# Rounding float64 weights to float32 without the second VectorE operation: bias taken off by ScalarE's scale, sign multiplied by GpSimd, no clamp

## The chip, the cores and the metric

The kernel runs on one core of a Trainium2 chip. A core has TensorE (PE in the profile: matmuls and transposes; PEld is its loading of weights), VectorE (DVE), ScalarE (ACT), GpSimd (POOL) and the DMA queues, here issued by SyncE (SP). Each engine works through its own instructions in program order and waits by semaphores for what other engines have to deliver first. The metric is the device time of one execution in microseconds (us), the median of several runs.

## The reference, cut to what matters

Attention in which each query keeps only its 32 largest scores, and behind it a feed-forward block with a gate:

```python
q, k, v: (8, 8, 576, 64) float32                    # batch, heads, sequence, head size
scores = (q @ k^T) / sqrt(64)
kth    = 32nd largest score of each row
attn   = softmax(where(scores >= kth, scores, -1e9))
x      = (attn @ v) laid out as (4608, 512)
g      = x @ w_gate                                 # w_gate, w_val: (512, 1536)
out    = (g * sigmoid(g) * (x @ w_val)) @ w_out     # w_out: (1536, 512)
```

`q`, `k` and `v` are float32. The three weights come out of NumPy as **float64**, because they are made by a product with a float64 number. The kernel computes in float32, so it has to round 2.36 million weights from 64 to 32 bits on the chip. That rounding is what the change is about.

## The kernel before

Work goes through the kernel in *units*: one unit is 128 queries of a pair of heads (both heads of 64 queries for the last rows). A unit's steps are spread over the engines and over later units, so that several units are in flight:

```python
def scores(n):      # TensorE: q k^T into PSUM; ScalarE: copies it to sc        (L304/L318, L309/L323)
def select(n):      # VectorE: top 32 by four rounds of max8 + match_replace    (L339, L343)
        nc.vector.tensor_scalar(                    # FAR for what lies below the 32nd        (L349)
            e[:, hs], sc[:, hs], m[:, t, TOP_K - 1 : TOP_K], FAR, ALU.is_lt, ALU.mult)
def penalize(n):    # GpSimd: e = e + sc                                        (L361)
def weigh(n):       # ScalarE: exp with row sums                                (L370)
def normalize(n):   # VectorE: reciprocal (L382); ScalarE: e * 1/sum            (L385)
def turn(n):        # TensorE: transposes of e (L397); ScalarE: copies (L398)
def values(n):      # TensorE: e v (L417, L426); ScalarE: copies to xT          (L441)
def feed(kb):       # feed-forward for 256 rows: L480 gate and value, L505-L513 on ScalarE and GpSimd,
                    # L526 or L566 with w_out; fed into the units' TensorE stream piece by piece
```

The rounding of the weights goes beside the first units. A piece is 128 x 512 weights; there are 24 pieces of `w_gate` and `w_val` and 12 of `w_out`. A float64 is two 32-bit words. The high word holds the sign, the 11 bits of the exponent and the upper 20 bits of the mantissa; the float32 needs those 20 bits and 3 more from the low word, rounded:

```python
def rounded(src, dst):
    w = ffn.tile([P, 2, WP, 2], I32, tag="w", name="w", bufs=3)
    nc.sync.dma_start(w[:].rearrange("p c f t -> p c (f t)"), src.bitcast(I32))           # L108
    yield
    low, high = w[:, :, :, 0], w[:, :, :, 1]
    size = conv.tile([P, 2, WP], FP32, tag="size", name="size", bufs=3)
    nc.scalar.activation(size[:], high.bitcast(FP32), AF.Abs)                              # L115
    nc.scalar.mul(low, low.bitcast(U32), 2.0**-29)         # top 3 bits, rounded            L117
    yield
    nc.gpsimd.tensor_scalar(size[:], size[:], HUGE, LEAST, ALU.min, ALU.max)               # L120
    yield
    bits = size[:].bitcast(I32)
    nc.vector.tensor_scalar(
        bits, bits, 3, 0x3FFFFFFF, ALU.logical_shift_left, ALU.bitwise_and)                # L124
    nc.gpsimd.tensor_tensor(bits, bits, low, ALU.add)                                      # L127
    yield
    nc.vector.scalar_tensor_tensor(                        # sign and top exponent bit
        out=dst.bitcast(I32), in0=high, scalar=-0x40000000, in1=bits,
        op0=ALU.bitwise_and, op1=ALU.bitwise_or)                                           # L130
```

`yield` parts a piece into stages. The stages of successive pieces are interleaved, a step of this loop after about every 2.2 of VectorE's selection instructions:

```python
    lags = (5, 3, 2, 2, 0)
    for n in range(2 * len(pieces) - 1 + lags[0]):
        for k, lag in enumerate(lags):
            if (n - lag) % 2 == 0:
                upto((n - lag) // 2, len(lags) - k)        # piece, stage
        ready[0] = max((n - lags[0]) // 2 + 1, 0)
        early[0] = lambda: upto(n // 2, 2)
        yield
```

`early[0]()` is called in each unit ahead of its exponentials, so that ScalarE's part of a piece need not wait behind them. The order of the rest of a unit:

```python
for n in range(NU + VALUES):
    ...
    penalize(n - 1); run(turn(n - 3)); finish_unit(n - 4)     # finish_unit calls values
    next(nxt, None)                  # scores(n + 1): TensorE
    early[0]()
    weigh(n - 1)
    run(nxt)                         # scores(n + 1): ScalarE's copies to sc
    dve(2, ...); pieces(2); dve(1); dve(1); run(norm); ...    # select(n), rounding, feed-forward pieces
```

Of the kernel before, what the change touches and what calls it, by code (L numbers as in the profile page):

```python
# [8 lines left out]
AF = mybir.ActivationFunctionType  # L9
ALU = mybir.AluOpType  # L10
FP32 = mybir.dt.float32
I32 = mybir.dt.int32
# [7 lines left out]
EPS = 1.0e-9  # L20
BLK = 256
WP = 256
HUGE = 122880.0
LEAST = 3.0517578125e-05


@with_exitstack
def kernel(
# [37 lines left out]
    nc = tc.nc  # L66
# [11 lines left out]
    scale = 1.0 / float(D) ** 0.5  # L78
# [26 lines left out]
    def rounded(src, dst):  # L105

        w = ffn.tile([P, 2, WP, 2], I32, tag="w", name="w", bufs=3)
        nc.sync.dma_start(  # L108
            w[:].rearrange("p c f t -> p c (f t)"), src.bitcast(I32)
        )  # L110
        yield
        low, high = w[:, :, :, 0], w[:, :, :, 1]

        size = conv.tile([P, 2, WP], FP32, tag="size", name="size", bufs=3)
        nc.scalar.activation(size[:], high.bitcast(FP32), AF.Abs)  # L115

        nc.scalar.mul(low, low.bitcast(U32), 2.0**-29)  # L117
        yield

        nc.gpsimd.tensor_scalar(size[:], size[:], HUGE, LEAST, ALU.min, ALU.max)  # L120
        yield

        bits = size[:].bitcast(I32)
        nc.vector.tensor_scalar(  # L124
            bits, bits, 3, 0x3FFFFFFF, ALU.logical_shift_left, ALU.bitwise_and
        )
        nc.gpsimd.tensor_tensor(bits, bits, low, ALU.add)  # L127
        yield

        nc.vector.scalar_tensor_tensor(  # L130
            out=dst.bitcast(I32), in0=high, scalar=-0x40000000, in1=bits,
            op0=ALU.bitwise_and, op1=ALU.bitwise_or,
        )

    def weights():


        pieces = []
        for f in range(0, DFF, WP):
            for src, dst in ((w_gate, wg), (w_val, wv)):  # L140
                for c in range(0, KC, 2):
                    rows = src[c * P : (c + 2) * P, f : f + WP]
                    pieces.append((
                        rows.rearrange("(c p) f -> p c f", p=P), dst[:, c : c + 2, f : f + WP]
                    ))
        for c in range(MC):
            pieces.append((
                w_out[c * P : (c + 1) * P].rearrange("p (c f) -> p c f", c=2),
                wo[:, c].rearrange("p (c f) -> p c f", c=2),
            ))  # L150
        pieces = [rounded(*p) for p in pieces]
        step = [0] * len(pieces)

        def upto(i, k):

            while 0 <= i < len(pieces) and step[i] < k:
                next(pieces[i], None)
                step[i] += 1


        lags = (5, 3, 2, 2, 0)
        for n in range(2 * len(pieces) - 1 + lags[0]):
            for k, lag in enumerate(lags):
                if (n - lag) % 2 == 0:
                    upto((n - lag) // 2, len(lags) - k)
            ready[0] = max((n - lags[0]) // 2 + 1, 0)
            early[0] = lambda: upto(n // 2, 2)
            yield
        early[0] = lambda: None


        add, sub = ALU.add, ALU.subtract
        lo, hi = slice(0, DM // 2), slice(DM // 2, DM)
        room = []
        for _ in range(3):
            t = ffn.tile([P, 4, DM // 2], FP32, tag="w", name="t", bufs=3)
            room += [t[:, 0:2], t[:, 2:4]]
        for m in range(0, MQ, 2):
            mm, nn = slice(m, m + 2), slice(MQ + m, MQ + m + 2)
            t3 = room.pop()  # L180
            nc.gpsimd.tensor_tensor(t3, wo[:, nn, hi], wo[:, mm, hi], sub)
            T[7] += [t3[:, i, :] for i in range(2)]
            yield
        while not plain_done:
            yield
        for m in range(0, MQ, 2):
            mm, nn = slice(m, m + 2), slice(MQ + m, MQ + m + 2)
            t1 = wo[:, mm, hi]
            nc.gpsimd.tensor_tensor(t1, t1, wo[:, mm, lo], sub)
            T[5] += [wo[:, m + i, hi] for i in range(2)]  # L190
            yield
            t2 = room.pop()
            nc.gpsimd.tensor_tensor(t2, wo[:, nn, hi], t1, sub)
            T[6] += [t2[:, i, :] for i in range(2)]
            yield
            t4 = conv.tile([P, 2, DM // 2], FP32, tag="size", name="t4", bufs=3)
            nc.gpsimd.tensor_tensor(t4[:], wo[:, nn, lo], t2, sub)
            T[4] += [t4[:, i, :] for i in range(2)]
            yield
        T[1] += [wo[:, m, lo] for m in range(MQ)]  # L200
        T[2] += [wo[:, MQ + m, lo] for m in range(MQ)]
        T[3] += [wo[:, MQ + m, hi] for m in range(MQ)]
        yield

    ready = [0]
    early = [lambda: None]
    plain_done = []
    T = {i: [] for i in range(1, 8)}
    weight = weights()

    def rounding(n):
# [46 lines left out]
    def prep(i):  # L258

        kq, kq_last = raw.pop(i)  # L260
        slab = slabs.tile([P, R + S + S], FP32, tag="kqT", name="kqT")
        for n, at in ((0, R), (None, S), (1, S + 2 * R)):
            ps = ps_t.tile([P, 512], FP32, tag="t", name="kqps")
            if n is None:
                nc.tensor.transpose(
                    ps[:, 0:P], kq_last[:].rearrange("p h d -> p (h d)"), ident[:]
                )
                nc.scalar.copy(slab[:, at : at + P], ps[:, 0:P])
                nc.scalar.copy(slab[:, 0:R], ps[:, 0:R])
                yield  # L270
                continue
            for c in range(J):
                nc.tensor.transpose(  # L273
                    ps[:, c * P : (c + 1) * P],
                    kq[:, n, c].rearrange("p h d -> p (h d)"),
                    ident[:],
                )
            nc.scalar.copy(slab[:, at : at + JP], ps[:])  # L278
        preps[i] = slab
# [8 lines left out]
    def scores(n):  # L288
        b, qt, hp = units[n]
        slab = preps[b * NHP + hp]  # L290
        sc = work.tile([P, 2 * S], FP32, tag="sc", name="sc", bufs=2)
        halves = [slice(0, D), slice(D, P)]
        half = S // 2

        def bank():
            return ps_t.tile([P, 512], FP32, tag="t", name="s")


        if qt == J:
            banks = [bank() for _ in range(2)]  # L300
            for i, ps in enumerate(banks):
                for d in halves:
                    k0 = R + i * half
                    nc.tensor.matmul(  # L304
                        ps[d, 0:half], slab[d, S + R : S + 2 * R], slab[d, k0 : k0 + half]
                    )
            yield
            for i, ps in enumerate(banks):
                nc.scalar.copy(sc[:, i * half : (i + 1) * half], ps[:, 0:half])  # L309
        else:  # L310
            q0 = S + 2 * R + qt * P
            banks = []
            for i in range(2):
                for hh, d in enumerate(halves):
                    ps = bank()
                    banks.append((i + 2 * hh, ps))
                    k0 = (1 - hh) * R + i * half
                    nc.tensor.matmul(  # L318
                        ps[:, 0:half], slab[d, q0 : q0 + P], slab[d, k0 : k0 + half]
                    )  # L320
            yield
            for i, ps in banks:
                nc.scalar.copy(sc[:, i * half : (i + 1) * half], ps[:, 0:half])  # L323
        state[n] = dict(sc=sc)
# [345 lines left out]
    def fetch(n):  # L670

        b, qt, hp = units[n]
        i = b * NHP + hp
        if qt == 0:
            yield from prep(i)
        if qt == J and i + NHP < len(pairs):
            load(i + NHP)
# [19 lines left out]
    def run(steps):  # L697
        for _ in steps:
            pass
# [9 lines left out]
    load(1)  # L709
    run(fetch(0))  # L710
    run(scores(0))
    run(fetch(1))
    credit = [0.0]
    no = iter(())
# [110 lines left out]
```

## Time and profile before

The time before is 1839.21 us (median of 3 runs, 1839.05 to 1842.51). The profiled execution has a span of 1835.9 us from its first to its last instruction.

| engine | busy us | share of span | instructions |
|---|---|---|---|
| PE | 1705.2 | 93% | 10756 |
| PEld | 1406.3 | 77% | 10756 |
| DVE | 1618.9 | 88% | 3405 |
| ACT | 1202.6 | 66% | 2943 |
| POOL | 1013.0 | 55% | 932 |

A share over the whole span is a mean over stretches with different limits. The rounding lies in the first eighth: its first ScalarE instruction starts at 12.9 us and its last VectorE instruction at 223.7 us. So views of single stretches say more than this table: a table of stretches gives, for each window, its length and each engine's busy time within it with the number of instructions, then the granted TensorE clock (1.00 is full speed), the share of DMA and its rate. In views of groups a line reads: line of the kernel, engine, operation, output and inputs with their shapes, count, then total busy time and mean time of one, and after that the idle time ahead of it with what ended it. A wait reads `waiter <- what it waited for: total us, times, longest`.

The instructions of the rounding, with the median time of one:

| line | engine | what | count | median ns |
|---|---|---|---|---|
| L115 | ACT | size from the high word | 36 | 676 |
| L117 | ACT | low word scaled | 36 | 674 |
| L120 | POOL | clamp | 36 | 612 |
| L124 | DVE | shift and mask | 36 | 426 |
| L127 | POOL | sum with the low bits | 36 | 1292 |
| L130 | DVE | sign and top bit put in | 36 | 680 to 686 |

### The profile page before, as it was taken

The numbers are of one execution on the slowest core, as the hardware profiler recorded it, in microseconds if no ns is written. First come the engines' busy times: TensorE is split into PE (matmuls) and PEld (weight loads), VectorE is DVE, ScalarE is ACT, GpSimd is POOL, SyncE is SP. The second block draws the span as 40 slices with busy tenths as digits, with TensorE's granted clock in tenths as the row PEclk, the third lists the DMA queues.
The fourth block names the chain that finished last, engine by engine and source line by source line (L and its number), as shares of the span: only waits on it lengthen the run. The fifth ranks groups of instructions, "written<-read, shape, count | busy, mean of one in ns | idle before, by whom it ended". The sixth has DMA issues, their size and how long they took to land.

```text
span 1835.9 us, 30517 instructions
## 1 busy us (share of the span) xinstructions
PE 1705.2 (93%) x10756; PEld 1406.3 (77%) x10756; DVE 1618.9 (88%) x3405; ACT 1202.6 (66%) x2943; POOL 1013.0 (55%) x932
## 2 busy tenths in 40 slices
PE   3448999999999989999999999999999999999998
PEld 2336758777888878887888878888788878888887
DVE  7999999999999889997999989998999989998300
ACT  5667766677666667666767676767776766675431
POOL 3556746645555545655464646564556554646444
PEclk7668999999999999999999999999999999999999
DMA  7332121000200021000300012000300011000000
GB/s 189 98 84 91 59 66 26 12 1 21 73 1 12 2 66 27 12 1 15 73 19 1 12 42 52 1 12 2 74 19 12 1 36 32 1 12 12 1 13 12
DMA packets 109145, 59.65 MB, mean 32 GB/s; under 512 B 88512, under 2 KB 96704, under 8 KB 108992
## 3 DMA queue, kind: packets, MB, share of 16 engines
q1 hardware_dynamic: 107936, 57.44, 12.1%
q8 instruction: 85, 1.39, 0.3%
q14 instruction: 68, 0.56, 0.1%
q10 hardware_dynamic: 1056, 0.26, 0.1%
HBM read 48.23 MB, written 9.44 MB: 31 GB/s over the span
## 4 chain that ended last, share of the span: by engine, by line
PE 83%; DVE 3%; POOL 2%; ACT 2%; issue 2%; POOLq 0%; ACTq 0%
PE f L480 39%; PE x_ps L566 9%; PE av L426 8%; PE etps L397 7%; PE s L318 7%; PE y_ps L566 7%; PE s L304 2%; PE av L417 1%; DVE m L339 1%; PE kqps L273 1%; DVE rest L343 1%; PE o_ps L526 1%; POOL e L361 1%; POOL p L552 0%; ACT e L370 0%
## 5 line engine op out<-in xcount | busy, mean ns | idle before, releaser
L339 DVE MAX8 m<-rest 128x8 f32<-128x576 f32 x864 | 619.3, 758 | 2.2
L343 DVE MATCH_REPLACE8 rest<-m,rest 128x576 f32<-128x576 f32 x576 | 427.1, 754 | 0.0
L361 POOL TENSOR_TENSOR e<-e,sc 128x1152 f32<-128x1152 f32 (+1 forms) x160 | 382.7, 2392 | 79.7 <-DVE e L349 61.0
L480 PE MATMUL f<-xT,wg 128*128 128x256 f32 x1728 | 401.6, 382 | 0.0
L480 PE MATMUL f<-xT,wv 128*128 128x256 f32 x1728 | 400.4, 382 | 0.0
L480 PEld LDWEIGHTS f<-xT,wg 128*128 128x128 f32 x1728 | 323.0, 190 | 62.6 <-issue 21.0
L480 PEld LDWEIGHTS f<-xT,wv 128*128 128x128 f32 x1728 | 325.3, 190 | 59.5 <-issue 16.6
L508 POOL TENSOR_TENSOR h<-h,half_g 128x512 f32<-128x512 f32 x108 | 138.1, 1279 | 295.6 <-ACT h L507 295.1
L339 DVE MAX8 m<-sc 128x8 f32<-128x576 f32 x288 | 206.4, 757 | 105.8 <-ACT sc L309 57.9
L370 ACT ACTIVATE e<-e,bias 128x576 f32<-128x576 f32 x288 | 222.1, 777 | 89.5 <-POOL e L361 89.5
L397 PE MATMUL etps<-ident,e 128*128 128x128 f32 (+1 forms) x1312 | 184.0, 285 | 96.9 <-POOL size L120 40.8
L398 ACT COPY et<-etps 128x512 f32<-128x512 f32 (+1 forms) x448 | 184.4, 484 | 124.6 <-PE etps L397 123.6
L397 PEld LDWEIGHTS etps<-ident,e 128*128 128x128 f32 (+1 forms) x1312 | 158.3, 146 | 124.3 <-POOL size L120 43.3
L513 POOL TENSOR_TENSOR h<-h,val 128x512 f32<-128x512 f32 x108 | 139.9, 1295 | 186.0 <-ACT val L512 185.8
L385 ACT ACTIVATE e<-e,tot 128x576 f32<-128x576 f32 x288 | 211.9, 789 | 7.0 <-DVE tot L382 6.7
L343 DVE MATCH_REPLACE8 rest<-m,sc 128x576 f32<-128x576 f32 x288 | 213.0, 750 | 0.0
L318 PE MATMUL s<-kqT 64*128 64x288 f32 x1024 | 171.6, 445 | 5.8 <-ACT kqT L278 3.6
L349 DVE TENSOR_SCALAR e<-sc,m 128x576 f32<-128x576 f32 x288 | 171.8, 640 | 3.4
L426 PE MATMUL av<-et,v 128*64 128x128 f32 (+1 forms) x2560 | 172.4, 280 | 0.0
L323 ACT COPY sc<-s 128x288 f32<-128x288 f32 x512 | 163.9, 402 | 1.8 <-PE s L318 1.7
L426 PEld LDWEIGHTS av<-et,v 128*64 128x64 f32 x2560 | 135.7, 144 | 22.7 <-issue 6.6
L505 ACT ACTIVATE h<-f 128x512 f32<-128x512 f32 x108 | 65.3, 605 | 130.9 <-PE f L480 130.9
(71 smaller groups left out, 2010.0 us busy)
## 6 DMA issues: line engine op xcount, KB each, us to landing
v<-in_v_dram SPq DMA_DIRECT2D x32, 256.0 KB, 3.0
kq_in<-in_k_dram SPq DMA_DIRECT2D x63, 128.0 KB, 3.0
kq_in<-in_q_dram SPq DMA_DIRECT2D x63, 128.0 KB, 3.0
w<-in_moe_w_gate_dram SPq DMA_DIRECT2D x12, 512.0 KB, 3.7
w<-in_moe_w_val_dram SPq DMA_DIRECT2D x12, 512.0 KB, 3.8
w<-in_moe_w_out_dram SPq DMA_DIRECT2D x12, 512.0 KB, 3.6
out_dram<-o SPq DMA_DIRECT2D x40, 128.0 KB, 2.4
out_dram<-o SPq DMA_DIRECT2D x16, 256.0 KB, 2.4
```

The lines of the kernel that those rows point to most:

```text
L318: nc.tensor.matmul(ps[:, 0:half], slab[d, q0 : q0 + P], slab[d, k0 : k0 + half])
L339: nc.vector.max(m[:, t, 8 * r : 8 * r + 8], cur[:, hs])
L343: nc.vector.match_replace(rest[:, hs], m[:, t, 8 * r : 8 * r + 8], cur[:, hs], LOWEST)
L349: nc.vector.tensor_scalar(e[:, hs], sc[:, hs], m[:, t, TOP_K - 1 : TOP_K], FAR, ALU.is_lt, ALU.mult)
L361: nc.gpsimd.tensor_tensor(e[:, every], e[:, every], sc[:, every], ALU.add)
L370: nc.scalar.activation(e[:, hs], e[:, hs], AF.Exp, bias=bias[:, t : t + 1], scale=scale, accum_out=tot[:, t : t + 1],)
L385: nc.scalar.mul(e[:, hs], e[:, hs], tot[:, t : t + 1])
L397: nc.tensor.transpose(ps[0:kl, c * P : (c + 1) * P], e[:, k0 : k0 + kl], ident[:])
L398: nc.scalar.copy(et[0:kl, c0 : c0 + cn, :], ps[0:kl, 0 : cn * P].rearrange("p (c j) -> p c j", c=cn),)
L426: nc.tensor.matmul(av[hh * R : (hh + 1) * R, 0:ql], v_last[:, hh, :] if c == J else vt[:, hh, c, :], moving, start=last and c == 0, stop=c ...
L480: nc.tensor.matmul(ps[:, i, :], w[:, kc, m * P : (m + 1) * P], x[:, kc, :], start=(kc == 0), stop=(kc == KC - 1),)
L566: nc.tensor.matmul(ps, lhsT, T[i][m], start=m == 0, stop=m == MQ - 1)
```

## The change

The change takes a different way from the two words to the float32. The high word, read as a float32, holds the float64's exponent in a field three bits too high, with a bias of its own. Multiplying by 2^-112 takes that bias off, so that a shift by 3 puts a right float32 exponent in place and no top bit has to be put back. ScalarE's instruction for the absolute value has a scale in it anyway. What is left is the sign: ScalarE computes it from the high word (plus or minus one, over the high word itself), and GpSimd multiplies it in as it writes the weight. VectorE's last operation and GpSimd's clamp go; without the clamp, weights beyond the range of float32 would no longer be held at its ends. The aim is to free VectorE of one of its two operations on each piece.

The stages become three, and ScalarE's part of the first piece is called ahead of the transposes of the second pair of heads. `ready` counts the pieces as before.

```diff
@@ def rounded(src, dst):
-        low, high = w[:, :, :, 0], w[:, :, :, 1]
+        low, high = w[:, :, :, 0], w[:, :, :, 1].bitcast(FP32)
         size = conv.tile([P, 2, WP], FP32, tag="size", name="size", bufs=3)
-        nc.scalar.activation(size[:], high.bitcast(FP32), AF.Abs)
+        nc.scalar.activation(size[:], high, AF.Abs, scale=2.0**-112)
         nc.scalar.mul(low, low.bitcast(U32), 2.0**-29)
+        nc.scalar.sign(high, high)
         yield
-        nc.gpsimd.tensor_scalar(size[:], size[:], HUGE, LEAST, ALU.min, ALU.max)
-        yield
         bits = size[:].bitcast(I32)
-        nc.vector.tensor_scalar(
-            bits, bits, 3, 0x3FFFFFFF, ALU.logical_shift_left, ALU.bitwise_and
-        )
+        nc.vector.tensor_single_scalar(bits, bits, 3, ALU.logical_shift_left)
         nc.gpsimd.tensor_tensor(bits, bits, low, ALU.add)
-        yield
-        nc.vector.scalar_tensor_tensor(
-            out=dst.bitcast(I32), in0=high, scalar=-0x40000000, in1=bits,
-            op0=ALU.bitwise_and, op1=ALU.bitwise_or,
-        )
+        nc.gpsimd.tensor_tensor(dst, size[:], high, ALU.mult)
@@ def weights():
-        lags = (5, 3, 2, 2, 0)
-        for n in range(2 * len(pieces) - 1 + lags[0]):
+        lags = (3, 2, 0)
+        for n in range(2 * len(pieces) + 4):
             for k, lag in enumerate(lags):
                 if (n - lag) % 2 == 0:
                     upto((n - lag) // 2, len(lags) - k)
-            ready[0] = max((n - lags[0]) // 2 + 1, 0)
+            ready[0] = max((n - 5) // 2 + 1, 0)
@@ start of the program
     run(scores(0))
+    early[0]()
     run(fetch(1))
```

More of the change, by code (lines that the diff above doesn't have):

```diff
@@ L22 @@
 WP = 256
-HUGE = 122880.0
-LEAST = 3.0517578125e-05
 @with_exitstack
```

## The prediction

> **What bounds the kernel now.** I first read the table of stretches, cut where the rounding passes from the 24 pieces of `w_gate` and `w_val` to those of `w_out` (155 us), where the rounding has ended (226 us), and where VectorE has nothing more to do (1720 us).
>
> ```profile
> 14.00:155.00 141.00, 55.55 (x323) 43.50 (x321) 139.73 (x296) 89.49 (x205) 79.18 (x71) 0.65 0.42 116
> 155.00:226.00 71.00, 69.14 (x393) 54.47 (x390) 70.87 (x142) 52.87 (x118) 49.88 (x43) 0.97 0.22 68
> 226.00:1720.00 1494.00, 1465.01 (x9417) 1210.13 (x9416) 1399.29 (x2948) 1017.61 (x2530) 828.55 (x752) 0.99 0.09 23
> ```
>
> Busy times stand in the order PE, PEld, DVE, ACT, POOL. In the first stretch VectorE is busy for 139.7 of 141 us while TensorE has work for only 55.6: VectorE alone sets the pace. In the second both are full (VectorE 70.9, TensorE 69.1 of 71). From 226 us on TensorE has 1465 of 1494 us, 98%, and VectorE 94%: TensorE sets the pace, with VectorE close behind. The shares of the whole chain agree (TensorE 83% of the span, VectorE 3%), but the chain of the first 240 us is nearly all VectorE.
>
> Next the groups of VectorE within the first 225 us, because what the change takes away stands there.
>
> ```profile
> L349 DVE TENSOR_SCALAR e<-sc,m 128x576 f32<-128x576 f32 x31 | 20.8, 712 | 0.0
> L124 DVE TENSOR_SCALAR size<-size 128x512 int32<-128x512 int32 x36 | 16.4, 457 | 3.3 <-POOL size L120 3.3
> L130 DVE SCALAR_TENSOR_TENSOR wo<-w,size 128x512 int32<-128x512 int32 x12 | 9.8, 817 | 0.1
> L130 DVE SCALAR_TENSOR_TENSOR wv<-w,size 128x512 int32<-128x512 int32 x12 | 8.3, 688 | 0.0
> L130 DVE SCALAR_TENSOR_TENSOR wg<-w,size 128x512 int32<-128x512 int32 x12 | 8.2, 687 | 0.0
> ```
>
> L130 is 26.3 us in all. VectorE waits next to nothing: 3.3 us for the clamp, 2.3 of them ahead of the very first piece. Last, two stretches of the order of time, on VectorE and GpSimd (start, duration, then the instruction):
>
> ```profile
> 50.62 0.94 DVE L349 TENSOR_SCALAR e<-sc,m 128x576 f32<-128x576 f32 x2
> ...
> 63.97 2.00 DVE L349 TENSOR_SCALAR e<-sc,m 128x576 f32<-128x576 f32 x2
> 64.21 1.44 POOL L127 TENSOR_TENSOR size<-size,w 128x512 int32<-128x512 int32 x1 [1.83 <-ACT xT L441]
> ```
>
> The same two instructions take 0.94 us when GpSimd runs none of its large operations, and 2.00 us when they meet its L127: they end only just after it has. VectorE's busy time thus hides waiting for GpSimd.
>
> [...] L349 (one tensor, 0.47 us of 576 columns when alone) and L130 of `wo` (two tensors, 817 ns against 687) are stretched, while max8 stays near 750 ns throughout. [...] In the built programs no load is added beside the one that stands in the trace (1.28 us at 2.07 us), so the sign costs only itself.
>
> **The change, part by part.** Setting the instruction streams of both programs side by side: TensorE's is the same instruction for instruction; VectorE's has 36 fewer, ScalarE's 36 more, GpSimd's as many as before, with each clamp replaced by a product.
>
> *VectorE.* 36 x L130 go: 24 x 0.687 = 16.5 us in the first stretch and 9.8 in the second. The shift alone costs what shift and mask did (0.43 us; one instruction over the same columns). The wait for the clamp goes: the shift now follows ScalarE's absolute value directly. Of the 3.3 us, 2.3 lie ahead of the first piece, whose ScalarE part is moved up, 1.0 ahead of two later ones; all in the first stretch.
>
> *GpSimd.* The clamp (0.612 us) becomes a product. Products of two 128 x 512 float32 tiles take 1279 ns (L508), so 36 x (1.28 - 0.61) = 24.1 us are added: 79.2 + 24 x 0.67 = 95 of 141 us in the first stretch, 50 + about 8 in the second. In the first it is beside other work, but it makes longer the time in which VectorE's L349 and shifts can meet GpSimd. L349's 15.5 pairs would take 15.5 x 0.94 = 14.6 us alone and take 20.8, so meeting costs 6.2 us now. GpSimd's time on the rounding grows from 36 x 1.90 = 68 to 36 x 2.57 = 93 us, and sum and product now come back to back after a shift, often just ahead of L349. I choose 4 us more, between a proportional 2.2 and a doubling: 2.5 in the first stretch, 1.5 in the second.
>
> *ScalarE.* 36 signs at 0.675 us, as L117, are 24.3 us: 89.5 + 16 = 106 us in the first stretch, which would be some 124 us long: 85%, room enough. Its delays reach VectorE only through `sc`, and the copies of a unit end some 6.4 us before VectorE needs them (in the order of time, copies from 43.74 to 45.02 us and the max8 on them at 51.46).
>
> *Second stretch.* Here VectorE could save 9.8 us, but TensorE has only 71 - 69.1 = 1.9 us of idle time. ScalarE would have 52.9 + 10 x 0.69 = 60 us, GpSimd 58 us of a stretch that VectorE alone would make 61 us long; in order and with waits (ScalarE sat 10.3 us waiting for L361 here) neither can be 95% busy. I give this stretch 3 us, less the 1.5 of meeting.
>
> *Afterwards* nothing is added or removed, TensorE's order is the same and it is the limit: the lead it has at 226 us should reach the end unchanged.
>
> Sum: first stretch 16.5 + 3.3 - 2.5 = 17.3; second 3 - 1.5 = 1.5; together 18.8 us. 1839.2 - 18.8 = 1820.4 us, 1.0% less.
>
> **The rivals.**
>
> 1. *All of it arrives.* 26.3 + 3.3 = 29.6 us, 1810 us. For it: after 226 us there are windows in which VectorE is again full while TensorE idles (340 to 380 us: 40.0 against 32.4 of 40), where a larger lead of VectorE could be used. Against it: TensorE is full in the second stretch, and between 240 and 260 us VectorE idles 2.5 of 20 us waiting for scores, which gives back a lead that TensorE doesn't share.
>
> 2. *ScalarE or GpSimd becomes the limit.* If the second stretch becomes longer by ScalarE's whole 6.9 us, and meeting GpSimd costs 8 instead of 4, then 16.5 + 3.3 - 5 in the first and -7 to -3 in the second are left: 8 to 12 us, about 1829 us. For it: exponentials already wait for L361 (19.0 us between 14 and 158 us), and sum and product now stand ahead of L361 in GpSimd's order. Against it: `sc` comes 6.4 us early.
>
> 3. *Hidden anyway.* The lead is lost to TensorE's 98% later: 1839 us. Against it: TensorE idles 85 us in the first stretch, and that idle time is what VectorE's pace sets. Its work can't be late for want of time there.
>
> 4. *Transfers.* Weights must land before ScalarE's part; ScalarE waited 18.1 us for them between 14 and 158 us, as a buffer comes free only when a piece is done. If the product comes late on GpSimd, these waits grow. I expect no more, since a piece now ends two steps of the loop earlier.
>
> **Range and chances.** Centre 1820.4 us. The low end, 1811, is nearly all of the first rival; the high end, 1833, is the second with something over. A gain over 2% needs 36.8 us, more than VectorE's whole removed work and waits: 2%. A loss over 2% needs GpSimd's products to hold up every unit by more than 2 us beyond what L130 gave back, or a slow sign: 2%. Within 2%: 96%.
>
> **What would show it.** Right, if: VectorE's rounding is 36 shifts of about 430 ns and nothing else; VectorE stays full until the rounding ends, and it ends near 205 us instead of 224; the clamp's waits are gone; L349 in that time is near 840 ns (20.8 + 4 us over 31) instead of 712; ScalarE's and GpSimd's new rows show 675 and 1280 ns; TensorE's busy time is the same within some us and its idle time in the first stretch is shorter by about the gain. Wrong, if: VectorE waits for `sc` or for ScalarE's absolute value by more than 5 us in the first 210 us; the shift takes much longer than 430 ns; the second stretch gets longer than 71 us; or the lead at the rounding's end differs from that at the end of the program by over 5 us.

## The result and the profile after

The changed kernel takes **1824.58 us** (median of 4 runs, 1823.24 to 1824.84) against 1839.64 us before on the same chip: a ratio of 0.9917, with a 95% interval from 0.9902 to 0.9931. That is 15.1 us less, where 18.8 had been predicted.

The table of stretches of the changed kernel, with the same cuts as before (PE, PEld, DVE, ACT, POOL):

```profile
14.00:155.00 141.00, 68.47 (x378) 53.82 (x379) 140.34 (x288) 107.72 (x244) 99.69 (x73) 0.64 0.43 124
155.00:226.00 71.00, 68.12 (x387) 50.95 (x386) 69.23 (x131) 59.34 (x133) 61.78 (x48) 0.98 0.18 54
226.00:1720.00 1494.00, 1468.55 (x9448) 1216.59 (x9447) 1390.38 (x2930) 1016.94 (x2528) 823.56 (x748) 0.99 0.09 23
```

VectorE is still busy for nearly all of the first 155 us, though 24 of its operations have gone from there. TensorE gets through 12.9 us more of its work in that time (68.5 against 55.6 us). The groups of VectorE in the first 225 us show what filled the gap (L339 is the mask, L349 before; L121 the shift, L124 before):

```profile
L339 DVE TENSOR_SCALAR e<-sc,m 128x576 f32<-128x576 f32 x33 | 31.0, 977 | 0.1
L121 DVE TENSOR_SCALAR size<-size 128x512 int32<-128x512 int32 x36 | 19.0, 528 | 2.0 <-ACT size L114 1.8
```

The mask went from 712 to 977 ns in the mean, the shift from 457 to 528. The order of time, on VectorE and GpSimd, shows the meeting that does it (start, duration, instruction):

```profile
70.87 1.29 POOL L122 TENSOR_TENSOR size<-size,w 128x512 int32<-128x512 int32 x1 [1.18 <-ACT w L116]
71.33 2.61 DVE L339 TENSOR_SCALAR e<-sc,m 128x576 f32<-128x576 f32 x2
72.24 1.38 POOL L123 TENSOR_TENSOR wv<-size,w 128x512 f32<-128x512 f32 x1
```

A pair of masks that takes 0.94 us alone takes 2.61: it begins within GpSimd's sum (L122) and ends at 73.94, just after the product (L123) has ended at 73.62. This meeting costs 1.67 us, the rest of the sum and the product behind it; of the 16 pairs before the 17th unit, 14 took 1.52 to 2.67 us.

VectorE's waits in the first 300 us, other than these hidden ones, are small (waiter, what it waited for: total us, times, longest):

```profile
DVE m L329 <- ACT sc L313: 11.5, 3, 9.3
DVE size L121 <- ACT size L114: 1.8, 3, 1.2
```

Of the 11.5 us, 9.3 are the start of the program, which the kernel before had too. For ScalarE's scores and absolute values VectorE waits some 4 us in all.

**An account of VectorE.** Reported durations overlap the start of the next instruction (before, a max8 is reported with 752 ns in the mean and takes 665 from start to start, less waits), so for sums I take times from start to start, read off the trace, from the first max8 to the first max8 of the 17th unit. Before, that is 215.3 us, after 202.7, so 12.6 us less. L130 is -24.3, the mask +8.8 (19.8 to 28.6), the shift +3.0 (13.2 to 16.2), all else together -0.1. The shift's part comes mainly from seven of the 36, all after 158 us: four of these meet products of the feed-forward on GpSimd (L498, L503) and none of the rounding's instructions, the other three its sum or its product.

**The lead.** As TensorE runs the same instructions in the same order in both kernels, the start of its n-th one can be subtracted. The lead grows to 10.1 us at 164 us of the old time and 14.3 at 244; it is 11.3 from 660 to 1500 and 12.8 at the end of the profiled executions. The medians are 15.1 us apart: the profiled execution of the kernel before, with 1837.67 us, was 2.0 us faster than its median.

### The profile page after: what moved, and what is told of

The parts are those of the page before. It is cut to its first block, busy times and chain, and to the rows that moved or that the text cites. A ratio compares the mean times of both kernels' runs of the same rounds, so it can differ in the third digit from the quotient of the medians.

```text
span 1823.1 us, 30504 instructions
## 1 busy us (share of the span) xinstructions
PE 1706.4 (94%) x10756; PEld 1408.2 (77%) x10756; DVE 1608.6 (88%) x3369; ACT 1220.7 (67%) x2979; POOL 1037.4 (57%) x932
## 4 chain that ended last, share of the span: by engine, by line
PE 84%; DVE 7%; ACT 4%; POOL 3%; issue 2%; DMA 0%; SPq 0%; POOLq 0%; DVEq 0%; ACTq 0%
PE f L470 40%; PE x_ps L556 9%; PE av L416 8%; PE etps L387 7%; PE s L308 7%; PE y_ps L556 7%; DVE m L329 3%; DVE rest L333 2%; PE s L294 2%; PE av L407 1%; DVE e L339 1%; PE kqps L263 1%; PE o_ps L516 1%; POOL e L351 1%; ACT e L360 1%
## 5 line engine op out<-in xcount | busy, mean ns | idle before, releaser
L498 POOL TENSOR_TENSOR h<-h,half_g 128x512 f32<-128x512 f32 x108 | 138.3, 1280 | 297.8 <-ACT h L497 291.2
L503 POOL TENSOR_TENSOR h<-h,val 128x512 f32<-128x512 f32 x108 | 139.5, 1292 | 189.5 <-ACT val L502 189.3
L339 DVE TENSOR_SCALAR e<-sc,m 128x576 f32<-128x576 f32 x288 | 179.2, 659 | 3.4
```

The costliest lines, as they stand in the source:

```text
L339: nc.vector.tensor_scalar(e[:, hs], sc[:, hs], m[:, t, TOP_K - 1 : TOP_K], FAR, ALU.is_lt, ALU.mult)
```

## The experiments

Three theories were told apart. Theory 1 (meeting): what is missing of VectorE's gain is its mask and shift waiting for GpSimd. Theory 2: ScalarE's signs hold things up. Theory 3: TensorE, full from 155 us on, caps the lead. Their results stand together here; the mask and the shift from start to start, the lead of TensorE over the kernel before at 244 us of the old time and at the end of the profile. The kernel before took 1839.78 us beside the runs without the product, the sign and L130 and beside spaced, and 1839.05 beside the last three. In spaced and in before, spaced, four shifts (in the latter five of L130 as well) still stand behind the start of the 17th unit.

| kernel | mask ns | shift ns | 17th unit begins, us | lead at 244 | lead at end | time us |
|---|---|---|---|---|---|---|
| before | 620 | 366 | 225.8 | 0 | 0 | 1839.64 |
| after | 894 | 449 | 213.5 | 14.3 | 12.8 | 1824.58 |
| no product | 626 | 371 | 201.0 | 26.4 | 23.5 | 1814.1 (one run) |
| no sign | 893 | 450 | 213.2 | 14.5 | 12.8 | 1824.82 (one run) |
| before, no L130 | 651 | 373 | 206.9 | 19.2 | 17.3 | 1820.31 (one run) |
| spaced | 469 | 517 | 197.7 | 23.8 | 18.1 | 1819.5 |
| spaced, full rate | 530 | 546 | 202.6 | 23.5 | 23.4 | 1816.0 |
| odd mask | 946 | 424 | 214.8 | 13.0 | 11.7 | 1825.98 (one run) |
| before, spaced | 424 | 403 | 214.8 | 1.3 | -4.4 | 1842.12 (one run) |

### The changed kernel without the product

The sign is left out of the weights.

```diff
-        nc.gpsimd.tensor_tensor(bits, bits, low, ALU.add)
-        nc.gpsimd.tensor_tensor(dst, size[:], high, ALU.mult)
+        nc.gpsimd.tensor_tensor(dst.bitcast(I32), bits, low, ALU.add)
```

> The changed kernel without GpSimd's product: its sum writes the weight itself, so the sign is left out (ScalarE still computes it). Theory 1 (meeting: the missing part of VectorE's gain is its mask and shift waiting for GpSimd's sum and product): the mask's mean falls from 977 ns to 700 or less, the shift's from 528 to about 440, and VectorE reaches the first max8 of its 17th unit at 198 to 204 us instead of 213.5. Theory 2 (ScalarE's signs hold things up): no more than 2 us change there, since the signs remain. Theory 3 (TensorE, full from 155 us on, caps the lead): VectorE gets there early but TensorE's lead at 244 us of the old time stays near the 14.3 us that it has in the changed kernel.

The group of the mask in the first 225 us of this run:

```profile
L339 DVE TENSOR_SCALAR e<-sc,m 128x576 f32<-128x576 f32 x35 | 23.5, 707 | 0.3
```

Mask and shift are where they were before the change (626 and 371 ns from start to start, against 620 and 366), and the 17th unit begins 12.5 us earlier than in the changed kernel. TensorE's lead at 244 us is 26.4 us. Theory 1 holds, and theory 3 falls: TensorE gains 10 us more after 164 us (16.4 to 26.4), 4.4 of them by 226 us, in the stretch that I held to be full, and 5.6 just behind it. The same instructions of TensorE in that stretch, before and in this run:

```profile
155.00:226.10 71.10, 69.24 (x394) 54.49 (x391) 70.97 (x142) 52.87 (x118) 49.88 (x43) 0.97 0.22 68
138.70:205.30 66.60, 66.60 (x394) 53.66 (x391) 65.80 (x138) 58.74 (x131) 47.73 (x36) 1.00 0.22 71
```

The 1.9 us of idle time are gone, and the busy time too is 2.6 us shorter, at a granted clock of 1.00 instead of 0.97.

### The changed kernel without the sign

The product multiplies by the raw high word, so the weights get a wrong size.

```diff
-        nc.scalar.sign(high, high)
```

> The changed kernel without ScalarE's sign: the product multiplies by the high word as it is, read as a float32, so weights get a wrong size; all else is the same. Theory 1: no change beyond 2 us in VectorE's time at its 17th unit (213.5 us) and the mask stays near 977 ns. Theory 2: ScalarE is 24 us freer, VectorE and TensorE are 4 to 8 us earlier by 244 us. Theory 3: as theory 1.

1824.82 us, with the lead at 244 us 0.2 us off that of the changed kernel. Leaving out ScalarE's 36 signs of 0.68 us brought nothing; theory 2 falls. The sign brought no load of tables either: the traces before and after each hold one ACT_TABLE_LOAD of ScalarE, 1.28 us at 2.07 us.

### The kernel before without L130

Sign and top exponent bit are left out, clamp and all else are kept.

```diff
-        nc.gpsimd.tensor_tensor(bits, bits, low, ALU.add)
+        nc.gpsimd.tensor_tensor(dst.bitcast(I32), bits, low, ALU.add)
         yield
-        nc.vector.scalar_tensor_tensor(
-            out=dst.bitcast(I32), in0=high, scalar=-0x40000000, in1=bits,
-            op0=ALU.bitwise_and, op1=ALU.bitwise_or,
-        )
```

> The kernel before with nothing but VectorE's last operation L130 taken out (GpSimd's sum writes the weight; sign and top exponent bit are left out), clamp and all else kept. Theory 1: the removal alone is worth 24 us on VectorE (24.3 us from start to start in the profile of before), the mask stays at 650 to 800 ns, and VectorE's 17th unit begins at 201 to 204 us. Theory 2: the same. Theory 3: TensorE's lead at 244 us of the old time is no more than 17 us, however early VectorE is.

The mask kept its length (651 ns) as theory 1 said, but the 17th unit begins at 206.9, not 201 to 204 us, and the lead at 244 us went past theory 3's 17. The waits of VectorE up to 226 us in this run say part of why:

```profile
DVE m L339 <- ACT sc L323: 9.1, 1, 9.1
DVE size L124 <- POOL size L120: 5.8, 6, 2.2
```

Waits for the clamp grew from 3.3 to 5.8 us: a quicker VectorE runs into GpSimd's clamp, which stands between ScalarE and the shift. Of the 5.4 us missing from the expected 24.3, 2.5 are these longer waits and 1.0 are waits that the 24.3 had counted as L130's; the mask takes 1.0 more. Taking out L130 alone is worth 18.9 us on VectorE; without the product it is 24.8, and the smaller waits there make up most of the difference. In that kernel the clamp is gone and ScalarE's part of the first piece, with 2.2 of the 5.8 us, is moved up; no run parts the two.

### Fixed places for the rounding

The same instructions, nothing left out, but no shift in the last five steps ahead of the mask:

```diff
+    rounding(1)                                  # once, ahead of the first unit
-                due[0] += 5 / 11 if beside else 0
-                if due[0] >= 1:
-                    due[0] -= 1
-                    rounding(1)
+                due[0] += 1                      # set to 0 at the start of each unit
+                if due[0] in ((5, 9) if nh == 2 else (3,)):
+                    rounding(2)
```

> The changed kernel with the rounding called twice in each unit at fixed places (after the 5th and the 9th of 14 selection steps) instead of after every 2.2 steps, so that no shift lies in the last five steps ahead of the mask; GpSimd's sum and product have then ended when the mask comes. The same instructions, output as the reference's. Theory 1: the mask's mean falls from 977 ns to 500 to 600, the shift stays near 430, VectorE's 17th unit begins near 202 us, and the time is 1812 to 1817 us. Theory 2: no change by more than 2 us (1823 to 1827). Theory 3: the mask gets shorter, but the time stays at 1821 to 1825.

Theory 1's expectation held on VectorE (mask 469 ns, the 17th unit at 197.7, with four shifts of some 2 us in all still to come), except that the shift took 517 ns: from 149 us on it meets GpSimd's feed-forward products (L498, L503) and late sums and products in every unit. The time, 1819.5 us (ratio to before 0.9888, 0.9872 to 0.9905), missed it by 2.5. The order of time of this run shows a mask that meets nothing:

```profile
73.17 0.42 DVE L121 TENSOR_SCALAR size<-size 128x512 int32<-128x512 int32 x1
...
73.72 1.30 POOL L122 TENSOR_TENSOR size<-size,w 128x512 int32<-128x512 int32 x1 [0.52 <-ACT e L375]
75.11 1.30 POOL L123 TENSOR_TENSOR wv<-size,w 128x512 f32<-128x512 f32 x1
...
76.94 0.94 DVE L339 TENSOR_SCALAR e<-sc,m 128x576 f32<-128x576 f32 x2
```

Sum and product follow the shift as before, end at 76.41 us, and the pair of masks begins half a microsecond later and takes its 0.94.

Yet TensorE's lead was 26.7 us near 200 us of the old time and then fell to 18.6. Its waits between 200 and 420 us hold a new one:

```profile
PE etps L387 <- issue: 8.5, 3, 4.1
PE etps L387 <- ACT e L375: 6.9, 3, 3.4
PE o_ps L516 <- POOL wo L123: 2.9, 2, 1.9
```

The last line is TensorE waiting for weights, 2.9 of the 8.1 us that it lost. Two pieces a unit are slower than the former 2.25: the last shift stood at 211.8 us, later than the changed kernel's 208.1, although VectorE was 16 us ahead.

### Fixed places at the full rate

```diff
+    rounding(1)                                  # once, ahead of the first unit; steps starts at 3
+                at[0] += 1                       # set to 0 at the start of each unit
+                if steps[0] < 76:                # while pieces are left
+                    if at[0] in ((3,) if nh == 1 else (4, 7, 10) if n % 4 == 3 else (5, 9)):
+                        rounding(2)
+                        steps[0] += 2
+                    continue
                 due[0] += 5 / 11 if beside else 0
                 if due[0] >= 1:
                     due[0] -= 1
                     rounding(1)
```

> The fixed places of the spaced variant, at the changed kernel's full rate: in each fourth unit three shifts (after steps 4, 7 and 10) instead of two, and from the end of the rounding on the old pace of the loop for what follows it, so that the last piece of w_out and the matrices built from it come as early as in the changed kernel. TensorE's order is that of the changed kernel; output as the reference's. Theory 1 (meeting) with the reading that the spaced variant lost 8.6 us of TensorE's lead after 210 us because its last weights came late: TensorE's lead at 244 us is 24 to 29 us, the end keeps all but 2 us of it, 1813 to 1816 us. If the lead is lost for another reason (VectorE's and TensorE's own pace between 226 and 400 us), it ends again at 1818 to 1821.

**1816.0 us** (4 runs, 1814.25 to 1816.84; ratio 0.9874, 0.9858 to 0.9891), with nothing left out. It beats both kernels: its interval lies below the changed kernel's (0.9902 to 0.9931), each against the kernel before. The last shift stands at 196.6 us, TensorE waits no longer for weights, and of a lead of 23.5 us at 244 us 23.4 arrive at the end. Its mask in the first 225 us:

```profile
L339 DVE TENSOR_SCALAR e<-sc,m 128x576 f32<-128x576 f32 x35 | 20.3, 617 | 0.3
L121 DVE TENSOR_SCALAR size<-size 128x512 int32<-128x512 int32 x36 | 22.5, 624 | 0.0
```

The spacing moves a part of the meetings from the mask to the shift: from start to start the mask takes 11.7 us less than in the changed kernel and the shift 3.5 us more. With three pieces in a unit, a shift also meets the product of the piece ahead of it:

```profile
48.62 1.29 POOL L123 TENSOR_TENSOR wv<-size,w 128x512 f32<-128x512 f32 x1
49.09 1.10 DVE L121 TENSOR_SCALAR size<-size 128x512 int32<-128x512 int32 x1
```

Two things differ from the spaced kernel, the third piece in each fourth unit and the old pace after the rounding; which of them kept the lead wasn't parted.

### An odd number of columns

The two masks of a unit over 577 columns each, overlapping by a column to both sides of the border between the heads; one column of head 0 is compared with the limit of head 1. (The edit is shown with a name, `cols`, for the repeated expression.)

```diff
+            cols = hs if nh == 1 else slice(575, 1152) if t else slice(0, 577)
-                e[:, hs], sc[:, hs], m[:, t, TOP_K - 1 : TOP_K], FAR, ALU.is_lt, ALU.mult
+                e[:, cols], sc[:, cols], m[:, t, TOP_K - 1 : TOP_K], FAR, ALU.is_lt, ALU.mult
```

> The changed kernel with each of a unit's two masks over 577 columns instead of 576 (overlapping by a column at both sides of the heads' border; one column in a unit of two heads is compared with the other head's limit). [...] it takes 600 to 700 ns from start to start wherever it stands, against 894 in the mean of the changed kernel and 469 alone; VectorE then reaches its 17th unit 6 to 9 us earlier than the changed kernel (205 to 207 us), though later units pay 0.3 us each. If the rate doesn't depend on the count's being odd, nothing changes (894 ns, 213.5 us).

Nothing of what was hoped for: the mask took 946 ns from start to start, against 894 in the changed kernel, and the time is 1825.98 us. So an odd count didn't take the mask out of GpSimd's way here. That it might, with 600 to 700 ns, was a guess of mine that no run had shown.

### Fixed places in the kernel before

```diff
+    rounding(1)                                  # and the edit of the spaced kernel, on the old stages
```

> The kernel before, L130 and clamp kept, with its rounding at the fixed places of the spaced variant (after the 5th and 9th of 14 steps). Theory 1: the mask falls from 620 ns from start to start to about 470, which frees 5 us of VectorE over 32 masks; L130 still costs 24 us, so VectorE's 17th unit begins near 219 to 222 us, and of the 28.1 us by which the spaced changed kernel leads there, 20 to 24 us are the change's own. If spacing alone does it, the 17th unit begins before 210 us.

The mask falls to 424 ns, but the 17th unit begins earlier than I expected (214.8), since five of L130 and four shifts had not been run by then; the last shift stands at 233.6 us, the last L130 at 235.5, and the time is 1842.12. Here, as in the spaced kernel, two pieces a unit are too slow, so this run doesn't say what the old kernel would do with a spacing at full rate. How much of the best kernel's 1816.0 us is spacing that the old kernel could have had as well stays open.

## Why the prediction was right, and where it was not

The total lay inside the range, with 3.7 us less gained than the centre says. That it came so near is in part luck: the profiled executions differ by 12.8 us, 6.0 short of the centre, and the parts did worse.

- **What bounds the kernel**: right. VectorE's time set the pace before 226 us, and what TensorE led by then reached the end to within 3 us (14.3 to 12.8 in the profiles, 15.1 in the medians).
- **L130**: 26.3 us was the sum of reported durations; from start to start it was 24.3. The difference is the overlap with the next instruction, less the 1.0 us of waits that follow L130 and count in the 24.3.
- **Meeting GpSimd**: the step that failed. I chose 4 us between 2.2 and a doubling; the mask alone cost 8.8 and the shift, that I had left at 0.43 us, 3.0. I had seen that sum and product would stand back to back ahead of the mask, but the two estimates were scaled by GpSimd's busy time and not by where its instructions stand. A pair of masks that began within 2.8 us of a shift's start met one or both, whatever the mean load: in 14 of 16 units a pair took 1.5 us or more instead of 0.94 (before, in 6). So two of the prediction's own signs came out against it: the mask took 977 ns instead of some 840 (which was mis-summed as well: 20.8 + 4 us over 31 masks are 800 ns), the shift 528 instead of 430.
- **The first stretch**: 17.3 us predicted; VectorE's 12th unit, at 158 us of the old time, begins 10.7 us earlier, 6.6 us short.
- **The second stretch**: 1.5 us predicted, and VectorE gained 1.7 (10.7 at its 12th unit, 12.4 at its 17th). TensorE gained nothing there (10.1 us at 164, 10.0 at 226); its lead rose to 14.3 just behind the stretch, between 226 and 244 us, where it had idled 4.9 us in the kernel before, and now idled 2.3 on the same instructions and was busy 1.6 less. The reason given for the small figure was wrong all the same: without the product VectorE gained 7.3 us in the stretch and TensorE 4.4, then 5.6 behind it, so neither TensorE's 1.9 us of idle time nor the load of ScalarE and GpSimd was a cap. What came behind the stretch made up 2.1 of the 6.6 us missing from the first, and the loss told below took it away again.
- **The clamp's waits**: gone as predicted, and worth more than the 3.3 us in the old trace, because they would have grown (to 5.8 us without L130).
- **Rivals**: ScalarE as the limit is refuted (no sign). GpSimd as a cost to VectorE was the right half of the second rival, and larger than it said: 11.8 us instead of 8. ScalarE's waits for weights fell from 18.1 to 4.3 us; the prediction had expected no growth. Of the first rival's 29.6 us, 23.4 came through in the profile once the meetings were spaced.

The lead falls by 2.4 us between 338 and 408 us of the old time in the changed kernel, and in the one without the product, but not in the best kernel. The stretches that hold the same 400 or so instructions of TensorE, before, after and in the best kernel:

```profile
338.10:408.10 70.00, 62.44 (x404) 51.50 (x402) 69.99 (x152) 49.67 (x126) 31.28 (x28) 0.95 0.02 8
```

```profile
323.80:396.20 72.40, 64.90 (x404) 53.59 (x403) 72.38 (x157) 49.91 (x126) 33.67 (x29) 0.91 0.02 8
```

```profile
314.50:384.60 70.10, 62.41 (x404) 51.46 (x403) 70.09 (x152) 49.77 (x126) 31.44 (x28) 0.95 0.02 9
```

TensorE idles as long in all three (7.6, 7.5 and 7.7 us). The 2.4 us are busy time, 64.9 instead of 62.4, at a granted clock of 0.91 instead of 0.95. So the lead was not lost by waiting longer; why the clock was granted lower there, with as much idle time, stays open.

## What to carry to other kernels

Moving an operation from a full VectorE to a GpSimd with room can give part of the gain back: here 11.8 of the 24.3 us that L130 had taken, as VectorE's mask and shift (a tensor and a scalar; from start to start 894 ns instead of 620, and 449 instead of 366) waited out GpSimd's running instructions. Max8, that also reads one tensor, did not: in the changed kernel its reported mean is 740 ns beside the sum or the product and 743 with GpSimd idle. This waiting shows as a longer VectorE instruction, not as idle time: the 2.61 us of the pair shown above instead of 0.94 are all busy time. So look not only for room on the other engine, but for what of VectorE stands within its instructions' reach, and space the two: here the same instructions in other places brought 1816.0 instead of 1824.6 us. And add up times from start to start, and compare stretches by the same instructions, not by the same time.

## What the runs showed of the hardware that I had not expected

- The mask waited for the end of a whole instruction of GpSimd: before and after, the 0.94 us pair took 1.28 to 2.67 us in 23 units, where it met some 0.8 us or more of GpSimd's sum, product or clamp, by how much of these was still to run. It ended 0.31 to 0.33 or 0.74 to 0.75 us behind one of them. Four pairs that met the last 0.2 us or less of one took 0.93 to 0.94 us. Max8 and match_replace beside them kept their pace (665 and about 660 ns from start to start, less waits, before and after). Once in the kernel before it went the other way, the pair ran on with 0.97 us and GpSimd's sum took 1.86 us instead of 1.29:

```profile
116.69 0.97 DVE L349 TENSOR_SCALAR e<-sc,m 128x576 f32<-128x576 f32 x2
116.94 1.86 POOL L127 TENSOR_TENSOR size<-size,w 128x512 int32<-128x512 int32 x1 [2.49 <-ACT xT L441]
```

- Reported durations of VectorE differ between traces without a difference in pace: max8 has a mean of 742 ns after against 752 before in the first 225 us, while from start to start, less waits, both are 665 ns.
- VectorE's shift took about the same with and without a mask behind it: before, with both operations, the median is 336 ns from start to start; with the shift alone it is 332 ns in the changed kernel and 328 without the product.
